# One-hots of a token dispatch built from ranks, wide selections, column-quarter gate logits and waits in a planned order

## Chip, core and metric

The kernel runs on one core of a Trainium2 chip. Times are microseconds (us) of one execution, measured on the device. A lower time is better. The engines are TensorE (PE in the profile, PEld for its weight loads), VectorE (DVE), ScalarE (ACT), GpSimd (POOL) and SyncE (SP, which issues most of the DMAs).

## What is computed

Three parts stand one behind the other, all in float32. S is 576, B is 4, so there are 2304 tokens of 512 values.

```python
# 1. attention, 8 heads of 64, mask by blocks of 64 positions
x = softmax(mask(q @ k.T / 8)) @ v
# 2. a token mix: xk, xr are blends of x and the row before it
k = relu(xk @ w_k);  v = (k * k) @ w_v
y = sigmoid(xr @ w_r) * v
# 3. an expert layer with 8 experts
logits = y @ w_gate;  gate = sigmoid(y @ w_local)
for each batch, for each token in order:
    e = argmax(logits) if first token or gate < 0.5 else the expert of the token before
    out = softmax(logits)[e] * (relu(y @ w1[e]) @ w2[e])
```

## The kernel before

**Attention** goes by 68 units (a batch, a head and a half of its queries, and one unit for the first 64 queries of a batch). **The mix** goes by 9 groups of 256 tokens (`mix_stream`): 96 products with w_k (`acc<-xh,wkh` and the like in the profile), 24 with w_r (`acc<-wrh,xh`), 48 with w_v (`acc<-wvh,kkh`). Each float32 operand is split into a high and a low part, so a product is three matmuls. **The expert layer** goes by slots of 128 tokens of one expert (`slot`): a gather of 128 rows of y by an index list (POOL's indirect DMA, `gidx`), loads of w1 and w2 of that expert, splits of both into high and low parts (ACT writes the high part, DVE the low one: `attr`, `wkh`, `wvh`, `kkh` and their partners, 8 instructions of 128x1024 on each engine for a slot), transposes, two products, a scatter (`sidx`). 19 slots always run, and three small ones of 32 rows (`small_slot`) are put in between at the places of `BEFORE`. A tile's gathered rows are split too: `wrh` on ACT and `wrl` on DVE, three times a slot.

**Which token goes where** is worked out on the chip. After a tile of 128 tokens leaves the mix, `flip` transposes it and `logits` multiplies it with the 9 gate columns (`wg`): four float32 matmuls, each with 128x128 of the tile as stationary operand. `route_group` finds the expert of each token, a one-hot over the experts (`o_all`), and by a triangular product the token's rank within its expert (`rank_all`). After 7 groups `dispatch(True)` gives out the first 7 slots, and after 9 groups `dispatch(False)` the others and the small ones. It works out where each expert's slots begin (`base`, a multiple of 128), so that base plus rank is a position: its upper part is the slot, its lower 7 bits the row. To turn positions into index lists it takes, for each of 14 or 18 tiles, a one-hot of the row (`d_lh`), a one-hot of the slot (`d_sel`), the latter times three values of the token (`d_rhs`: its number and a two-part weight), and one matmul that adds them into one bank (`pinv`). Then `gidx`, `sidx` and `pslot` are read out of it.

**The order** on each engine is fixed ahead by a planner: every call is recorded with its cost, and `schedule` is a list scheduler that takes, for the engine that comes free first, the ready instruction with the lowest `prio` (the length of the work that hangs on it). Everything that is not of the expert layer stands ahead of it by `prio -= 1e5`. Nearly all instructions thus carry the line of the recording helper (L273 before), so the profile is read by tiles. Buffers are rings; `acc` has two banks, shared by all products of the mix.

## Time and profile before

| | us |
|---|---|
| median of 3 runs | 810.71 (809.32 to 812.0) |
| the profiled execution, its own time | 808.18 |
| its span in the profile | 806.4 |

The profiled execution lies 2.5 us under the median. Busy shares of the span: PE 96%, DVE 76%, ACT 66%, POOL 37%. A busy share is an average over stages: attention to about 137 us, attention beside the mix to 477 us, the end of the mix to 525.5 us, the expert layer to 796 us, and the last scatter.

### The profile page before, as it was taken

How to read it: one execution, taken by the hardware profiler on the slowest of the kernel's cores; microseconds unless marked ns; L12 is line 12 of the kernel's file. 1: busy time of each engine (PE TensorE's matmuls, PEld its weight loads, DVE VectorE, ACT ScalarE, POOL GpSimd, SP SyncE). 2: the span in 40 equal slices, each digit the busy share in tenths (PEclk: the TensorE clock that was granted, in tenths of full speed). 3: DMA queues.
4: the chain of work that ended last, by engine and by line, in shares of the span. 5: the costliest groups of instructions: out<-in, count | busy, mean ns of one | idle time of the engine just before them, and what ended most of it. 6: DMA issues, size and time to landing. Idle time of an engine off the chain costs nothing.

```text
span 806.4 us, 15002 instructions
## 1 busy us (share of the span) xinstructions
PE 778.0 (96%) x5040; PEld 640.3 (79%) x5040; DVE 609.6 (76%) x1346; ACT 535.3 (66%) x1156; POOL 299.9 (37%) x275
## 2 busy tenths in 40 slices
PE   8999999999999999999999997999989999999994
PEld 8665798988888989898998986767867777767773
DVE  6986767775789869576785479699999986866840
ACT  3888566983578946265893525469769977867841
POOL 3343585533656427345452332222121521312200
PEclk9999999999999999999999999899999999999998
DMA  8574312211233202201310005111475287695300
GB/s 216 161 211 153 106 57 82 88 45 35 77 92 99 72 17 83 76 28 37 99 45 14 14 27 209 40 39 40 144 248 197 66 275 268 213 327 187 120 15 23
DMA packets 40466, 87.62 MB, mean 109 GB/s; under 512 B 6540, under 2 KB 10640, under 8 KB 40384
## 3 DMA queue, kind: packets, MB, share of 16 engines
q1 hardware_dynamic: 37152, 76.71, 29.6%
q0 software_dynamic: 3232, 9.90, 3.5%
q8 instruction: 41, 0.67, 0.4%
q14 instruction: 41, 0.34, 0.1%
HBM read 131.68 MB, written 9.90 MB: 176 GB/s over the span
## 4 chain that ended last, share of the span: by engine, by line
PE 67%; issue 11%; DVE 11%; DMA 6%; ACT 2%; POOL 1%; SPq 1%; POOLq 0%; ACTq 0%; DVEq 0%
PE acc L273 38%; PE s L273 12%; PE psT L273 9%; PE av L273 6%; DMA out<-xm,sidx 2%; PE acc L1379 1%; DVE wvl L273 1%; DVE attr L273 1%; DVE xm L273 1%; DMA out<-v,ssum 1%; DVE wrl L273 1%; DMA wraw<-in_w 1%; DMA x<-in_w 1%; ACT attr L273 1%; DVE relu L273 1%
## 5 line engine op out<-in xcount | busy, mean ns | idle before, releaser
L273 DVE TENSOR_REDUCE nm<-s 128x1 f32<-128x576 f32 (+4 forms) x132 | 67.7, 547 | 24.2 <-ACT s L273 22.9
L273 PE MATMUL acc<-xh,wkh 128*128 128x256 f32 x288 | 82.1, 295 | 0.9 <-ACT xh L273 0.6
L273 PE MATMUL acc<-xl,wkh 128*128 128x256 f32 x288 | 82.0, 293 | 0.1
L1236 POOL DMA_INDIRECT out<-xm,sidx x19 | 26.3, 1383 | 147.6 <-ACT xm L273 124.9
L273 PE MATMUL acc<-xh,wkl 128*128 128x256 f32 x288 | 80.7, 289 | 0.0
L273 POOL TENSOR_TENSOR attr<-qk,attr 64x512 fp32r<-64x512 f32 (+1 forms) x48 | 65.7, 1368 | 37.8 <-ACT attr L273 30.3
L273 PE MATMUL av<-attr 128*128 128x256 f32 (+3 forms) x336 | 77.4, 288 | 0.8 <-ACT x L273 0.3
L273 DVE TENSOR_TENSOR attr<-psT,attr 64x256 fp32r<-64x256 f32 (+2 forms) x120 | 63.1, 526 | 17.1 <-ACT attr L273 14.7
L273 POOL TENSOR_TENSOR kkl<-relu,kkh 128x512 fp32r<-128x512 f32 x36 | 47.7, 1329 | 61.9 <-ACT kkh L273 53.6
L273 PE MATMUL s<-attr 128*128 128x288 f32 (+3 forms) x288 | 67.1, 300 | 0.6 <-ACT ea L273 0.6
L273 POOL TENSOR_TENSOR xl<-xm,xh 128x512 fp32r<-128x512 f32 x36 | 46.8, 1301 | 49.7 <-ACT xh L273 45.9
L273 ACT ACTIVATE attr<-psT 64x256 fp32r<-64x256 f32 (+2 forms) x120 | 53.0, 463 | 10.4 <-PE psT L273 9.5
L273 PE MATMUL acc<-attr,wrh 128*128 128x512 f32 x160 | 56.7, 405 | 1.1 <-ACT wrh L273 1.1
L273 ACT ACTIVATE xh<-xm 128x512 fp32r<-128x512 f32 x36 | 22.7, 631 | 52.0 <-DVE xm L273 51.9
L273 PE MATMUL acc<-wvh,kkh 128*128 128x512 f32 x144 | 56.6, 414 | 0.0
L273 PEld LDWEIGHTS acc<-xh,wkh 128*128 128x128 f32 x288 | 53.9, 191 | 2.9 <-ACT xh L273 0.9
L273 PEld LDWEIGHTS av<-attr 128*128 128x128 f32 (+1 forms) x336 | 51.5, 166 | 5.3 <-DVE x L273 0.7
L273 PE MATMUL acc<-wvl,kkh 128*128 128x512 f32 x144 | 55.5, 407 | 0.0
L273 PE MATMUL acc<-wvh,kkl 128*128 128x512 f32 x144 | 55.5, 408 | 0.0
L273 PEld LDWEIGHTS acc<-xl,wkh 128*128 128x128 f32 x288 | 54.2, 191 | 1.1 <-POOL xl L273 0.4
L273 PEld LDWEIGHTS acc<-xh,wkl 128*128 128x128 f32 x288 | 54.1, 191 | 0.4
L273 PE MATMUL psT<-ident,eb 128*128 128x128 f32 (+1 forms) x288 | 54.3, 278 | 0.0
(347 smaller groups left out, 2392.8 us busy)
## 6 DMA issues: line engine op xcount, KB each, us to landing
x<-in_w SPq DMA_DIRECT2D x76, 512.0 KB
eb<-in_w SPq DMA_DIRECT2D x38, 512.0 KB
qk<-in_qk SPq DMA_DIRECT2D x24, 544.0 KB
qk<-in_w SPq DMA_DIRECT2D x19, 512.0 KB
d<-in_w SPq DMA_DIRECT2D x19, 512.0 KB
wraw<-in_w SPq DMA_DIRECT2D x24, 256.0 KB
y_dram<-th SPq DMA_DIRECT2D x18, 256.0 KB
v<-in_v SPq DMA_DIRECT2D x28, 160.0 KB
```

Of the source, the lines that this page charges most:

```text
L273: o[2](*o[3], **o[4])
L1236: plan.add("pool", "scatter", lambda: nc.gpsimd.indirect_dma_start(out=out, out_offset=bass.IndirectOffsetOnAxis(ap=at.bitcast(U32), axis= ...
L1379: plan.warm = lambda: pe.matmul(first[:, 0:128], ones, ones, start=True, stop=True)
```

## The change

- **One-hots from ranks.** Since `base` is a multiple of 128, the row is the rank's lower 7 bits. `dispatch` builds all row one-hots from `rank_all` first, once a tile, in bf16, and keeps them: tiles 0 to 15 in the two `wraw` buffers, 16 and 17 in a new tile `hots`. The second dispatch builds four and reuses 14.
- **Wide selections.** One instruction gives the slot one-hots of all 14 tiles (6 tiles in the second dispatch), another multiplies them with the token's values. The values are five bf16 parts (token number in two, weight in three), so the matmuls are bf16 with 5w columns, and three sums put the parts together.
- **Logits.** The gate's weights, padded to 32 columns, are the stationary operand. Four matmuls, one for each 128 of the 512 values, write one quarter of the partitions each; ACT copies the bank to `lt`, PE transposes it, and DVE sums the four parts into `lg` (before, a copy).
- **The planner** lets ACT, DVE and POOL stand idle for at most 300 ns (and half of the instruction at hand) where an instruction that is much more urgent comes ready within that time. The second dispatch has the rank `late`, which loses the lead over the expert layer. The small slots move from places 10, 13 and 15 to 9, 12 and 18.

```diff
-BEFORE = (EARLY + 3, EARLY + 6, EARLY + 8)
+BEFORE = (EARLY + 2, EARLY + 5, EARLY + 11)
...
+FIRM, AHEAD, URGENT = ("act", "dve", "pool"), 300.0, 2000.0
...
-            i = heapq.heappop(b if b and (not a or b[0] < a[0]) else a)[1]
+            mine = b if b and (not a or b[0] < a[0]) else a
+        if e in FIRM and soon[e]:
+            r, j = soon[e][0]
+            if r < t + min(AHEAD, 0.5 * ops[mine[0][1]][2]) and prio[j] < mine[0][0] - URGENT:
+                free[e] = r
+                continue
+        i = heapq.heappop(mine)[1]
...
-        start, order = schedule([(o[0], o[5], o[6], o[8], o[9], o[7][0] != "ffn") for o in ops], until if self.warm else -1, 54.0)
+        start, order = schedule([(o[0], o[5], o[6], o[8], o[9], o[7][0] not in ("ffn", "late")) for o in ops], until if self.warm else -1, 54.0)
...
-    wg = cst.tile([128, 4, NE + 1], F32, name="wg")
+    wg = cst.tile([128, 4, ROWS], F32, name="wg")
+    pool.memset(wg, 0.0)
...
-            pl = aux()
-            for c in range(4):
-                pe.matmul(pl[:, 0:NE + 1], box["yT"][:, c * 128:c * 128 + 128], wg[:, c, :],
-                          start=(c == 0), stop=(c == 3))
-            dve.tensor_copy(lg[:, j, :], pl[:, 0:NE + 1])
+            pl, yt = aux(), box["yT"]
+            def issue():
+                for c in range(4):
+                    nc.tensor.matmul(pl[c * ROWS:c * ROWS + ROWS, 0:128], wg[:, c, :],
+                                     yt[:, c * 128:c * 128 + 128], start=True, stop=True)
+            plan.add("pe", "tiles", issue, outs=[pl[:, 0:128]], ins=[wg, yt], hold=230.0)
+            lt = ring(m1, "lt", [128, 128], F32, 1)
+            act.copy(lt, pl[:, 0:128])
+            pe.transpose(pl[:, 128:256], lt, ident)
+            dve.reduce_sum(lg[:, j, :], pl[:, 128:256].rearrange("p (c e) -> p e c", e=ROWS)[:, 0:NE + 1, :],
+                           axis=AX.X)
...
-    vals = rt.tile([128, NT, 3], F32, name="vals")
+    vals = rt.tile([128, NT, 5], BF16, name="vals")
+    hots = rt.tile([128, 2, 128], BF16, name="hots")
     es = rt.tile([1, SLOTS + 1], F32, name="es")
     dve.memset(es[:, 0:1], -1.0)
+    def hot(t):
+        if t >= 16:
+            return hots[:, t - 16, :]
+        x = buffers(a1, "wraw", [128, 512], F32, 2)[1 + t // 8].bitcast(BF16)
+        return x[:, t % 8 * 128:t % 8 * 128 + 128]
...
+        if not early:
+            plan.rank = ("late", 0, 0)
...
+        for t in ((slice(0, 12), slice(12, 14)) if early else (slice(14, 16), slice(16, 18))):
+            ri, rf = (small(x, [128, 12], dt)[:, 0:t.stop - t.start] for x, dt in (("ri", I32), ("rf", F32)))
+            dve.tensor_copy(ri, rank_all[:, t])
+            dve.tensor_scalar(ri, ri, 127, None, op0=ALU.bitwise_and)
+            dve.tensor_copy(rf, ri)
+            for i in range(t.start, t.stop):
+                dve.tensor_scalar(hot(i), iota128, rf[:, i - t.start:i - t.start + 1], None, op0=ALU.is_equal)
...
-        phr = small("phr", [128, NT], F32R)[:, ts]
-        dve.tensor_copy(phr, p_all[:, ts])
-        dve.tensor_scalar(vals[:, ts, 0], tok[:, ts], 1.0, None, op0=ALU.add)
-        dve.tensor_copy(vals[:, ts, 1], f(phr))
-        dve.tensor_tensor(vals[:, ts, 2], p_all[:, ts], f(phr), op=ALU.subtract)
+        v, x = vals[:, ts, :], f(small("phr", [128, NT], F32R)[:, ts])
+        y = posi[:, 0:v.shape[1]]
+        dve.tensor_scalar(y, tok[:, ts], 1.0, None, op0=ALU.add)
+        for i, mask in enumerate((0x7FFFFFF0, 15)):
+            z = x.bitcast(I32)
+            dve.tensor_scalar(z, y, mask, None, op0=ALU.bitwise_and)
+            dve.tensor_copy(v[:, :, i], z)
+        dve.tensor_copy(v[:, :, 2], p_all[:, ts])
+        dve.tensor_tensor(x, p_all[:, ts], v[:, :, 2], op=ALU.subtract)
+        dve.tensor_copy(v[:, :, 3], x)
+        dve.tensor_tensor(v[:, :, 4], x, v[:, :, 3], op=ALU.subtract)
...
-        for t in range(nt):
-            lh = ring(rt, "d_lh", [128, 128], F32R, 2)
-            dve.tensor_scalar(lh, iota128, pmd[:, 0, t:t + 1], None, op0=ALU.is_equal)
-            sel = ring(rt, "d_sel", [128, 22], F32, 2)[:, 0:w]
-            dve.tensor_scalar(sel, iota25[:, j0:j0 + w], pmd[:, 1, t:t + 1], None, op0=ALU.is_equal)
-            rhs = ring(rt, "d_rhs", [128, 66], F32R, 3)[:, 0:3 * w].rearrange("p (k w) -> p k w", k=3)
-            dve.tensor_tensor(rhs, sel.unsqueeze(1).to_broadcast([128, 3, w]),
-                              vals[:, t, :].unsqueeze(2).to_broadcast([128, 3, w]), op=ALU.mult)
-            pe.matmul(pinv[:, 0:3 * w], lh, rhs, start=(t == 0), stop=(t == nt - 1))
-        inv = small("inv", [128, 66])[:, 0:3 * w].rearrange("p (k w) -> p k w", k=3)
-        dve.tensor_copy(inv, pinv[:, 0:3 * w].rearrange("p (k w) -> p k w", k=3))
+        k = nt if early else 6
+        for t0 in range(0, nt, k):
+            t1 = slice(t0, t0 + k)
+            sel = small("sel", [128, 6 * 22], BF16)[:, 0:k * w].rearrange("p (t w) -> p t w", w=w)
+            dve.tensor_tensor(sel, iota25[:, j0:j0 + w].unsqueeze(1).to_broadcast([128, k, w]),
+                              pmd[:, t1].unsqueeze(2).to_broadcast([128, k, w]), op=ALU.is_equal)
+            rhs = small("rhs", [128, 6 * 110], BF16)[:, 0:k * 5 * w].rearrange("p (t i w) -> p t i w", i=5, w=w)
+            dve.tensor_tensor(rhs, sel.unsqueeze(2).to_broadcast([128, k, 5, w]),
+                              vals[:, t1, :].unsqueeze(3).to_broadcast([128, k, 5, w]), op=ALU.mult)
+            for t in range(k):
+                pe.matmul(pinv[:, 0:5 * w], hot(t0 + t), rhs[:, t].rearrange("p i w -> p (i w)"),
+                          start=(t0 + t == 0), stop=(t0 + t == nt - 1))
...
+        inv = small("inv", [128, 110])[:, 0:5 * w].rearrange("p (k w) -> p k w", k=5)
+        dve.tensor_copy(inv, pinv[:, 0:5 * w].rearrange("p (k w) -> p k w", k=5))
+        dve.tensor_tensor(inv[:, 0, :], inv[:, 0, :], inv[:, 1, :], op=ALU.add)
         dve.tensor_scalar(sidx[st], inv[:, 0, 0:n], -1.0, None, op0=ALU.add)
         dve.tensor_scalar(gidx[st], inv[:, 0, 0:n], -1.0, 0.0, op0=ALU.add, op1=ALU.max)
-        dve.tensor_tensor(pslot[st], inv[:, 1, 0:n], inv[:, 2, 0:n], op=ALU.add)
+        dve.tensor_tensor(inv[:, 1, :], inv[:, 2, :], inv[:, 3, :], op=ALU.add)
+        dve.tensor_tensor(inv[:, 1, :], inv[:, 1, :], inv[:, 4, :], op=ALU.add)
+        dve.tensor_copy(pslot[st], inv[:, 1, 0:n])
```

On DVE, from the cast of the positions (`d_pmd`) to the first index list (`gidx`), before. One tile's three selection instructions repeat, two tiles at a time, with weight splits (`attr<-...`) between them:

```order
L273 CAST d_pmd_185<-d_posi_184 128x2x14
L273 COPY lg_159<-s_0_133 128x9
L273 TENSOR_SCALAR d_sel_189<-iota_103,d_pmd_185 128x8
...
L273 TENSOR_SCALAR d_lh_187<-iota_104,d_pmd_185 128x128
L273 TENSOR_TENSOR d_rhs_191<-d_sel_189,vals 128x24
...
L273 TENSOR_TENSOR attr<-qk_131,attr 128x1024
...
L273 TENSOR_TENSOR attr<-x_0_119,attr 128x1024
L273 COPY d_inv_194<-av_140 128x24
L273 TENSOR_TENSOR wkl<-x_0_121,wkh 128x1024
L273 TENSOR_SCALAR gidx_109<-d_inv_194 128x7
```

The same place in the changed kernel (the instructions of `vals` and two of `xm` are left out):

```order
L282 CAST d_pmd_189<-d_posi_188 128x14
L282 TENSOR_SCALAR d_posi_188<-tok 128x14
L282 TENSOR_TENSOR d_sel_191<-iota_103,d_pmd_189 128x112
...
L282 SCALAR_TENSOR_TENSOR relu_127<-relu_127 128x512
...
L282 TENSOR_TENSOR d_rhs_169<-d_sel_191,vals 128x560
L282 SCALAR_TENSOR_TENSOR xm_129<-d_128,mu_r,x_1_123 128x256
...
L282 TENSOR_TENSOR evi_106<-es 1x7
...
L282 COPY d_inv_192<-av_141 128x40
...
L282 TENSOR_SCALAR gidx_109<-d_inv_192 128x7
```

The 42 selection instructions have become two, and no weight split stands ahead of `gidx` any more; `evi`, the list of experts that the weight loads wait for, now stands behind the selection (before, ahead of `d_pmd`).

On ACT, around the first two weight splits (`attr<-eb`), before:

```order
L273 ACTIVATE relu_126<-acc_151 128x512
L273 ACTIVATE kkh_156<-relu_126 128x512
L273 ACTIVATE attr<-eb_146 128x1024
L273 ACTIVATE attr<-eb_147 128x1024
L273 ACTIVATE relu_126<-acc_151 128x512
L273 ACTIVATE attr<-qk_131 128x1024
```

And in the changed kernel (`th<-acc` reads the first product with w_r out of its bank):

```order
L282 ACTIVATE relu_127<-acc_152 128x512
L282 ACTIVATE kkh_157<-relu_126 128x512
L282 ACTIVATE attr<-eb_147 128x1024
L282 ACTIVATE attr<-eb_148 128x1024
L282 ACTIVATE kkh_157<-relu_127 128x512
L282 ACTIVATE th_124<-acc_151 128x512
L282 ACTIVATE attr<-qk_132 128x1024
```

The reads of the products with w_k now all stand ahead of the two splits; the last `kkh` and the first `th` stand behind them.

On DVE, around the second index list (`gidx_110`, for slots 7 and up), before; the `wrl` behind it is the split of slot 5's gathered rows:

```order
L273 COPY d_inv_194<-s_0_133 128x66
L273 TENSOR_TENSOR xh_152<-x_0_121,kkh_156 128x1024
L273 TENSOR_SCALAR gidx_110<-d_inv_194 128x18
...
L273 COPY d_inv_194<-av_140 128x3
L273 TENSOR_TENSOR wrl<-psT_138,wrh 128x512
```

And in the changed kernel, where the `wrl` ahead of it is that of slot 6:

```order
L282 COPY d_inv_192<-s_0_134 128x110
L282 TENSOR_TENSOR wrl<-psT_140,wrh 128x512
...
L282 TENSOR_TENSOR wkl<-x_0_122,wkh 128x1024
L282 TENSOR_SCALAR gidx_110<-d_inv_192 128x18
```

Counted in slots, the second index list has moved back by more than one.

## Rows read from the trace of the kernel before

**Rows 1.** The page: span and instructions.

```profile
span 806.4 us, 15002 instructions
```

**Rows 2.** Windows by stage: length, busy us of each engine (instructions), clock, DMA share, GB/s.

```profile
137.00:477.00 340.00, 337.51 (x2362) 301.06 (x2360) 248.17 (x638) 218.40 (x585) 156.81 (x131) 0.99 0.18 57
477.00:525.50 48.50, 40.80 (x231) 34.67 (x230) 40.67 (x120) 24.33 (x33) 14.79 (x10) 0.89 0.32 115
525.50:604.20 78.70, 75.84 (x388) 59.66 (x388) 76.21 (x210) 57.20 (x76) 15.87 (x11) 1.00 0.34 118
604.20:796.00 191.80, 189.66 (x1110) 142.86 (x1110) 140.67 (x140) 141.86 (x190) 42.31 (x30) 1.00 0.53 178
```

**Rows 3.** Timeline of PE, 477 to 525.5: start, us, instruction, [idle before, releaser].

```profile
494.37 0.50 PE L273 MATMUL acc<-wrh,xh 128*128 128x512 f32 x1 [1.38 <-ACT relu L273]
...
501.74 0.68 PE L273 MATMUL av<-d_rhs,d_lh 128*128 128x24 f32 x2 [2.43 <-DVE d_rhs L273]
...
505.05 1.88 PE L273 MATMUL s<-wg,relu 128*128 128x9 f32 x8 [0.68 <-ACT relu L273]
...
525.45 0.74 PE L273 MATMUL acc<-attr,wrh 128*128 128x512 f32 x2 [1.06 <-ACT wrh L273]
```

**Rows 4.** Timeline of DVE, the first selection.

```profile
481.86 0.28 DVE L273 TENSOR_TENSOR d_ob<-o_all,taken 128x112 f32<-128x112 f32 x1
...
484.29 0.68 DVE L273 SCALAR_TENSOR_TENSOR relu<-relu 128x512 f32<-128x512 f32 x1
...
487.13 1.20 DVE L273 CAST d_pmd<-d_posi 128x28 f32<-128x28 int32 x1
...
489.96 0.23 DVE L273 TENSOR_SCALAR d_sel<-iota,d_pmd 128x8 f32<-128x8 f32 x1
...
490.38 0.28 DVE L273 TENSOR_SCALAR d_lh<-iota,d_pmd 128x128 fp32r<-128x128 f32 x1
...
504.26 0.15 DVE L273 TENSOR_SCALAR gidx<-d_inv 128x7 int32<-128x7 f32 x1
```

**Rows 5.** Timeline of ACT: a copy out of PSUM, and the first weight split.

```profile
466.01 0.37 ACT L273 COPY wraw<-av 64x256 f32<-64x256 f32 x1
...
491.42 1.06 ACT L273 ACTIVATE attr<-eb 128x1024 fp32r<-128x1024 f32 x1 [0.72 <-DMA eb<-in_w]
```

**Rows 6.** Timeline of PE, one tile's logits and the next instruction.

```profile
444.82 1.06 PE L273 MATMUL acc<-wg,relu 128*128 128x9 f32 x8
...
445.74 0.37 PE L273 MATMUL acc<-xl,wkh 128*128 128x256 f32 x1
```

**Rows 7.** Timeline of PE, a column-quarter product (line 1319) between full ones.

```profile
672.50 0.40 PE L273 MATMUL s<-wkl,wrh 128*128 128x512 f32 x1
...
672.74 0.40 PE L273 MATMUL acc<-attr,wrl 128*128 128x512 f32 x1
...
673.06 0.65 PE L1319 MATMUL av<-wraw,x 128*32 128x128 f32 x16
...
673.74 0.40 PE L1319 MATMUL av<-th,x 128*32 128x128 f32 x8
...
674.07 0.66 PE L273 MATMUL psT<-ident,ea 128*128 128x128 f32 x4
...
674.49 0.48 PE L273 MATMUL s<-wkh,wrl 128*128 128x512 f32 x1
```

**Rows 8.** Timeline of PE, the longest wait after 525.5.

```profile
604.18 0.50 PE L273 MATMUL s<-kkh,wrh 128*128 128x512 f32 x1 [2.09 <-ACT xm L273]
```

**Rows 9.** Timeline of DVE: x splits of slots 0 and 7, the second gather list.

```profile
525.96 0.68 DVE L273 TENSOR_TENSOR wrl<-psT,wrh 128x512 fp32r<-128x512 f32 x1
...
592.19 0.17 DVE L273 TENSOR_SCALAR gidx<-d_inv 128x18 int32<-128x18 f32 x1
...
623.30 0.69 DVE L273 TENSOR_TENSOR wrl<-psT,wrh 128x512 fp32r<-128x512 f32 x1
```

More of the change, by code (lines that the diff above doesn't have):

```diff
@@ L313, in load_constants @@
         sp.dma_start(wg[:, :, 0:NE], a["w_gate"].rearrange("(c p) e -> p c e", p=128))
-        sp.dma_start(wg[:, :, NE:], a["w_local"].rearrange("(c p) e -> p c e", p=128))
+        sp.dma_start(wg[:, :, NE:NE + 1], a["w_local"].rearrange("(c p) e -> p c e", p=128))
     o_all = cst.tile([128, NT, NE], F32, name="o_all")
@@ L932, in to_row @@
                 pe.transpose(v["pk"][0:1, j * 128:j * 128 + 128], v["key"][:, j:j + 1], ident)
-            scan = ring(rt, "scan", [1, GT], F32, 1)
+            scan = ring(rt, "d_rhs", [128, 6 * 110], BF16, 1).bitcast(F32)[0:1, 0:GT]
             init = 0.0 if scan_prev[0] is None else carry
@@ L1108, in dispatch @@
             dve.tensor_tensor(posf, posf, far, op=ALU.add)
-        posi = small("posi", [128, 2, NT], I32)[:, :, 0:nt]
-        dve.tensor_tensor(posi[:, 0, :], posf, rank, op=ALU.add)
-        dve.tensor_scalar(posi[:, 1, :], posi[:, 0, :], 7, None, op0=ALU.logical_shift_right)
-        dve.tensor_scalar(posi[:, 0, :], posi[:, 0, :], 127, None, op0=ALU.bitwise_and)
-        pmd = small("pmd", [128, 2, NT])[:, :, 0:nt]
+        posi = small("posi", [128, NT], I32)[:, 0:nt]
+        dve.tensor_tensor(posi, posf, rank, op=ALU.add)
@@ L1114, in dispatch @@
+        dve.tensor_scalar(posi, posi, 7, None, op0=ALU.logical_shift_right)
+        pmd = small("pmd", [128, NT])[:, 0:nt]
         dve.tensor_copy(pmd, posi)
         ts = slice(0, nt) if early else slice(EG * 2, NT)
-        phr = small("phr", [128, NT], F32R)[:, ts]
-        dve.tensor_copy(phr, p_all[:, ts])
-        dve.tensor_scalar(vals[:, ts, 0], tok[:, ts], 1.0, None, op0=ALU.add)
-        dve.tensor_copy(vals[:, ts, 1], f(phr))
-        dve.tensor_tensor(vals[:, ts, 2], p_all[:, ts], f(phr), op=ALU.subtract)
+        v, x = vals[:, ts, :], f(small("phr", [128, NT], F32R)[:, ts])
@@ L1139, in dispatch @@
+        dve.tensor_tensor(inv[:, 1, :], inv[:, 1, :], inv[:, 4, :], op=ALU.add)
+        dve.tensor_copy(pslot[st], inv[:, 1, 0:n])
         if not early:
             dve.tensor_scalar(gidx_s, inv[:, 0, n:m], -1.0, 0.0, op0=ALU.add, op1=ALU.max)
-            lh = ring(rt, "d_lh", [128, 128], F32R, 2)
+            lh = flat(hots).bitcast(F32)
             dve.tensor_copy(lh.rearrange("p (t r) -> p t r", r=ROWS),
@@ L1145, in dispatch @@
             pr = aux()
-            pe.matmul(pr[:, 0:3 * SMALLS], f(lh), inv[:, :, n:m], start=True, stop=True)
+            pe.matmul(pr[:, 0:2 * SMALLS], lh, inv[:, 0:2, n:m], start=True, stop=True)
             dve.tensor_scalar(sidx_s, pr[:, 0:SMALLS], 4.0, quarter, op0=ALU.mult, op1=ALU.add)
-            dve.tensor_copy(inv[:, 0, 0:SMALLS], pr[:, SMALLS:2 * SMALLS])
-            dve.tensor_tensor(pslot_s, inv[:, 0, 0:SMALLS], pr[:, 2 * SMALLS:3 * SMALLS], op=ALU.add)
+            dve.tensor_copy(pslot_s, pr[:, SMALLS:2 * SMALLS])
     def units():
```

2 lines of the change are left out of this document (1 added, 1 removed).

## Prediction, before the changed kernel was timed

> **What bounds the kernel now.** The span is 806.4 us [rows 1]; the execution's own time is 808.2 us, 1.8 more, and the median of the runs 2.5 above that. The first view is the table of windows by stage. From 137 to 477 us PE is busy 337.5 of 340 us, while DVE has 248 and ACT 218 [rows 2]: there PE sets the pace, and what leaves PE shortens the stage. From 525.5 on PE is busy again (75.8 of 78.7 and 189.7 of 191.8 us), though in the first of these stretches DVE, with 76.2 of 78.7, is as full as PE [rows 2]. The odd stretch lies between, 477 to 525.5 us: PE has 40.8 of 48.5 us and a mean granted clock of 0.89, where the stages around it have 0.99 and 1.00 [rows 2].
>
> The second view is PE's timeline there. It waits 1.38 us for ACT's read of a product, then 2.43 us for the selection of the first dispatch (`d_rhs`, DVE), later 1.06 us for the split of slot 0's rows [rows 3]. Behind the 2.43 us the logits take 1.88 us for what takes 1.06 elsewhere [rows 3, 6]: after the waits PE runs at the lower of its two levels, 1.2 instead of 2.4 GHz. The third view, DVE's timeline, says why the selection is late: from the cast of the positions at 487.13 to `gidx` at 504.26 pass 17.1 us [rows 4], in which DVE does 14 times three small instructions, with weight splits between.
>
> So the sum has three terms: PE work taken out of the saturated stage, the loss in 477 to 525.5, and what the expert layer gains or loses.
>
> **Term 1, the logits.** A tile's eight passes start at 444.82 and the next instruction at 445.74: 0.92 us [rows 6]. No logits of the new form are in the trace, but the small slots have the same shape of product (stationary 128x32, 128 columns, column quarters). There 32 passes start at 673.06, the last eight at 673.74: 0.028 us apart. The full product ahead of them would have freed PE at 672.98 (0.24 after 672.74, as the one before it), and the next one starts at 674.07, about 0.10 after the last pass could end [rows 7]. So entry and exit cost 0.18 us, and eight passes 0.23: 0.41. The added transpose costs a quarter of four, (674.49 - 674.07) / 4 = 0.105 [rows 7]. A tile falls from 0.92 to 0.52, 0.40 saved.
>
> The Trainium skill, "TensorEngine Tiling (Array Packing)", section "Theoretical Speedup", gives up to 4x for a dimension of at most 32, by which the block alone would be 0.92 / 4 = 0.23; its section "Key Properties" says that a change of tiling mode drains the engine. The 0.18 us at the edges agree with the second and speak against counting the first in full: by the 4x alone the term for 14 tiles would be 14 x (0.92 - 0.23 - 0.105) = 8.2 us.
>
> By the rows, 14 of the 18 tiles lie in the saturated stage: 14 x 0.40 = 5.6 us. What it adds on ACT, a copy of 128 columns from PSUM, is bounded by 0 and the 0.37 us of a copy of 256 columns [rows 5]; at 0.3, 18 are 5.4 us, on an engine idle for 120 us of that stage [rows 2]. If ACT set the pace this would cost up to those 5.4 us; the idle share says that it doesn't. DVE's copy becomes a sum of 36 values, below the 0.28 us of a 112-wide instruction [rows 4], hidden likewise. The chain of a tile grows by a copy and a transpose, under 1 us; nothing waits for it before the last tiles. I take 5 of the 5.6 us, with 0 as the lower bound.
>
> **Term 2, the first dispatch.** A tile's selection takes 0.42 us of DVE (489.96 to 490.38) [rows 4], 14 of them 5.9. In their place come one instruction of 112 elements (0.28, as `d_ob`) and one of 560, bounded by 0.28 and 1.06 (the 1024-wide split) [rows 4, 5] and nearest to the 512-wide one: 0.7 [rows 4]. To these come eight to ten small ones for the values and sums, at 0.15 at most 1.5. The row one-hots, each at most 0.28 (`d_lh`) [rows 4], 14 of them 3.9 at most and nearer 2.8 pipelined, are made ahead, in the gaps that DVE has while it waits for the last ranks. Five weight splits of 1.1 us and the waits for PE between the one-hots leave the path too. What stays behind the cast is two squares of 0.6, two or three `xm` of 0.4, the matmuls and some small ones: about 6 us for 17.1. `gidx` should come 11 us sooner. Against it, `evi` goes behind the selection, so the weight loads start some 4 us later than now; now the first split waited 0.72 us for its load at 491.42 [rows 5].
>
> What PE gets of these 11 us. Its loss in the stretch is 48.5 - 40.8 = 7.7 us of waits [rows 2], and of the clock's missing 0.11 x 48.5 = 5.3 us the part that falls on work, which I put at 3.5: 11.2 together. Its work also shrinks, by two logits (0.8) and 14 selection matmuls, now bf16 (0 to 0.1 each; 0.05 taken): 1.5. New waits: the order puts the first `th` on ACT behind two splits whose loads are late. The mix has two banks, so the first product with w_v must wait for that `th`, which I work out to come 2 us after PE wants the bank; and slot 0's split on ACT stands behind four or five splits of the next weights, which the end of the mix frees, as now (1.06 us) [rows 3]. So 3 us of new or remaining waits: 11.2 + 1.5 - 3 = 9.7, taken as 10. Bounds: 13 without new waits, 4 if the loads or the ACT queue hold the mix as long as the selection did.
>
> **Term 3, the expert layer.** PE saves two logits (0.8) and 18 selection matmuls (0.05 each, 0.9). The 2.09 us wait at 604 [rows 8], behind a stretch in which DVE was full with the second dispatch, may go: DVE loses 18 times at least 0.42 us and gets back four one-hots and six wide instructions, about 5, so 3 us less. Against that stands that the first products begin sooner with less in stock. By the order, 13 weight splits stood ahead of slot 0's rows on DVE and now 9: four splits, 4.5 us, that DVE must make up while it is full. Seven slots took 97.3 us from 525.96 to 623.30 [rows 9], 13.9 each. Between +3.8 (all gains, no cost) and -3 (no wait goes, the whole stock lost) I take +1. The small slots move; their places cost nothing now but short waits, and I take 0.
>
> The planner's short waits moved few instructions of the attention stage by more than a few places on any engine; at 2.5 us of waits of PE from 137 to 477 [rows 2] there is little to gain: 0, between -3 and +2.
>
> **Sum.** 5 + 10 + 1 = 16 us: 808.2 - 16 = 792.2 for the profiled execution, 794 to 795 for a median of such runs; I say 794.
>
> **Rivals.**
> (a) *The second list comes too late.* It now stands behind slot 6's split. Before, it came at 592.19 and slot 7's split at 623.30, 31 us ahead [rows 9]. Now a slot's length of about 12.4 us (48 products of 0.24 and twelve transposes of 0.105 [rows 7]) must hold the list, the gather and slot 7's transposes, which I estimate at 9. Each us beyond the 3 to 4 us of slack is one of PE, and more by the clock. It decides against the change from 20 us on: with DVE 24 us behind at slot 6, 794 + 20 = 814. DVE's 3 us less work speak against, its missing stock for it.
> (b) *The first stretch stays long.* The loads, 4 us later, and ACT's queue take the place of the selection, and term 2 falls to 4: 800. For it speaks the wait on a load at 491.42 [rows 5]; against it, that the two reads PE waits for most stand ahead of the splits now.
> (c) *PE's saved work turns into waits* in the mix stage, because ACT's copies hold its two banks: term 1 is 0, 799. Against: 120 us of idle ACT [rows 2].
> (d) *DVE limits slots 1 to 4*, at -3 for term 3: 798, or 803 with (c).
> (e) *Nothing comes of it*: the selection is short, but PE, in its fixed order, waits for another thing as long, and (c) holds: 809 to 811.
> (f) *Better*: the waits at 604 and those of the mix go too, 786 to 788.
>
> **Chances.** Forecast, 788 to 800 with (c) or (d) alone in part: 0.66. (b): 0.12. (c) and (d) in full: 0.06. (f): 0.07. (e): 0.03. (a) to the point of a loss: 0.06. A difference of 0.3% (2.4 us) is about what can be told from no change: faster 0.91, same 0.03, slower 0.06. The range reaches from the better case to (b) and (d) with (c): 786 to 804.
>
> **What would show it.** Right: logits of eight passes with 0.4 us to the next instruction; no wait of PE over 2 us for the selection between the first `d_sob` and slot 0's first product; `gidx` ahead of the first `attr` split; that stretch 10 us shorter, its granted clock over 0.95; the stage before it 5 us shorter. Wrong: PE waits for `th` or `kkh` behind weight splits for more than 3 us, waits on slot 7's gather, or a DVE without gaps up to slot 7 with PE waiting for `wrl` or its partners. The forecast fails most easily in term 2, since ACT's queue there rests on the landing of loads that I did not see in that place.

## The result and the profile after

The changed kernel takes 801.87 us (median of 6 runs, 799.13 to 803.61) against 811.36 us before (6 runs): a ratio of 0.9885, 95% interval 0.9858 to 0.9913. The forecast was 794 in a range of 786 to 804: faster, as said, but 9.5 us by the medians where 16.7 were forecast (810.71 - 794). The profiled execution took 800.13 us, 8.05 less than the one of before, half of the 16 that the prediction added up for it; the spans differ by 8.0 [rows 1].

```profile
span 798.4 us, 15016 instructions
```

To say where the 8 us came from, both kernels are cut at the same three instructions: the first logits, the first product with `d_sob`, and slot 0's first product; the last cut is the end of PE's last product. The windows of the kernel before (columns as in [rows 2]):

```profile
140.56:477.18 336.62, 334.13 (x2338) 297.87 (x2337) 244.88 (x630) 214.94 (x574) 154.99 (x130) 0.99 0.18 56
477.18:525.45 48.27, 40.57 (x230) 34.48 (x226) 40.45 (x119) 24.28 (x33) 14.73 (x10) 0.89 0.32 115
525.45:795.85 270.40, 265.55 (x1497) 202.57 (x1497) 216.93 (x350) 199.03 (x264) 58.22 (x41) 1.00 0.47 160
```

And of the changed kernel:

```profile
140.35:475.37 335.02, 330.00 (x2355) 288.74 (x2355) 244.26 (x640) 217.38 (x589) 155.99 (x129) 1.00 0.18 57
475.37:515.00 39.63, 34.83 (x227) 28.56 (x226) 32.74 (x92) 23.75 (x34) 12.92 (x10) 1.00 0.38 140
515.00:786.24 271.24, 263.87 (x1499) 201.02 (x1499) 219.43 (x323) 199.83 (x267) 55.85 (x40) 0.99 0.47 160
```

The mix stage gained 1.6 us where 5 were expected, the first dispatch 8.6 (expected 10), the expert layer lost 0.8 (expected +1), and from PE's last product to the end the kernel now takes 798.4 - 786.24 = 12.2 us instead of 806.4 - 795.85 = 10.6, which nobody had counted. With 0.2 at the start that is 8.0.

The mix stage first. PE has 4.1 us less work in it, and 335.02 - 330.00 = 5.0 us without work instead of 2.5. Some of the work is the clock's: before, PE ran at the lower of its two levels from 347.1 to 350.5 us, in the changed kernel nowhere in this stage. The timeline of PE shows a block of the new logits between other work:

```profile
246.27 0.42 PE L903 MATMUL acc<-relu,wg 128*32 128x128 f32 x8
246.63 0.40 PE L282 MATMUL av<-attr 128*64 128x256 f32 x2
```

0.36 us to the next instruction, where the old block took 0.92 [rows 6]. So each block is as short as forecast, and the stage is not. The trace lists what PE waits for here. The largest group, 1.5 us in five places, is the logits product itself, which waits for ACT's copy of the transposed tile, its own input; 0.8 us are waits for the reads behind it (`lt` on ACT, `lg` on DVE).

The first dispatch, on PE's timeline: the 14 selection products in one row, the two waits for `th`, slot 0's first product.

```profile
487.26 0.52 PE L282 MATMUL av<-d_rhs,wraw 128*128 128x40 bf16 x14
...
498.55 0.50 PE L282 MATMUL acc<-wvh,kkh 128*128 128x512 f32 x1 [1.61 <-ACT th L282]
...
504.77 0.51 PE L282 MATMUL acc<-wvh,kkh 128*128 128x512 f32 x1 [1.55 <-ACT th L282]
...
515.00 0.96 PE L282 MATMUL acc<-attr,wrh 128*128 128x512 f32 x3 [0.21 <-ACT wrh L282]
```

The 2.43 us wait for `d_rhs` [rows 3] is gone; 1.61 and 1.55 for `th`, behind ACT's weight splits, have taken its place, and the clock is 1.00 instead of 0.89. In all PE is without work for 4.8 us here, before for 7.7. On DVE the selection now looks like this:

```profile
481.97 0.17 DVE L282 CAST d_pmd<-d_posi 128x14 f32<-128x14 int32 x1
...
482.26 0.27 DVE L282 TENSOR_TENSOR d_sel<-iota,d_pmd 128x112 bf16<-128x112 f32 x1
...
484.53 1.79 DVE L282 TENSOR_TENSOR d_rhs<-d_sel,vals 128x560 bf16<-128x560 bf16 x1
...
490.71 0.16 DVE L282 TENSOR_SCALAR gidx<-d_inv 128x7 int32<-128x7 f32 x1
...
495.77 3.03 DVE L282 TENSOR_TENSOR attr<-eb,attr 128x1024 fp32r<-128x1024 f32 x2 [1.42 <-ACT attr L282]
```

From `d_pmd` to `gidx` it is 8.7 us, not 17.1 [rows 4], and the first weight split comes 5 us behind the list. Of the 17.1 us before, the 42 selection instructions took 8.1 (from the start of each to DVE's next instruction) and five weight splits 5.7; DVE was idle for only 0.8, in one wait for PE. The first split, and that wait:

```profile
492.71 1.22 DVE L273 TENSOR_TENSOR attr<-eb,attr 128x1024 fp32r<-128x1024 f32 x1
...
496.33 0.29 DVE L273 TENSOR_SCALAR d_lh<-iota,d_pmd 128x128 fp32r<-128x128 f32 x1 [0.81 <-PE av L273]
```

In the expert layer the 2.09 us wait at 604 [rows 8] has gone, and a longer one stands at slot 7:

```profile
600.80 0.39 PE L282 MATMUL s<-wkh,wrl 128*128 128x512 f32 x1
606.19 1.12 PE L282 MATMUL psT<-ident,ea 128*128 128x128 f32 x4 [5.01 <-DMA ea<-y_dram,gidx]
...
608.39 0.63 PE L282 MATMUL s<-wkl,wrh 128*128 128x512 f32 x1
608.82 0.58 PE L282 MATMUL s<-wkh,wrl 128*128 128x512 f32 x1
609.23 0.40 PE L282 MATMUL s<-wkh,wrh 128*128 128x512 f32 x1
```

PE waits 5.0 us for slot 7's gathered rows, and for some 3 us behind that a product takes 0.43 us instead of 0.23: the lower clock. The second gather list came at 595.58 us on DVE (592.19 before [rows 9]), but the split of slot 7's gathered rows has moved from 619.29 to 608.24, so 12.7 us lie between the two instead of 27.1. (A slot's three `wrl` are one split of its gathered rows and two of the two halves of its hidden values; the 623.30 of [rows 9] is one of the latter, of slot 6. By the same reading the list stood behind the rows of slot 5 before and stands behind those of slot 6 now: one slot, not more.) The split of slot 7's rows, before:

```profile
619.29 0.69 DVE L273 TENSOR_TENSOR wrl<-psT,wrh 128x512 fp32r<-128x512 f32 x1 [0.46 <-ACT wrh L273]
```

With the list another thing moved, which the prediction didn't name: `evi`, the list of experts by which SP picks the weights of slots 7 and up. DVE wrote it at 555 us before and now at 594:

```profile
594.27 0.16 DVE L282 TENSOR_TENSOR evi<-es 1x18 int32<-1x18 f32 x1
```

SP's weight loads around it, in the changed kernel:

```profile
569.88 21.07 SPq L1305 DMA_DIRECT2D x<-in_w  x3
593.63 0.37 SPq L1305 DMA_DIRECT2D d<-in_w  x1
597.13 0.99 SPq L1305 DMA_DIRECT2D eb<-in_w  x2
```

The first loads behind the new list start at 597.13, in the same microseconds in which the gather (issued at 596.51) has to land.

### The profile page after: what moved, and what is told of

Read it like the earlier page. It is cut to its first block, busy times and chain, and to the rows that moved or that the text cites. A ratio compares the mean times of both kernels' runs of the same rounds, so it can differ in the third digit from the quotient of the medians.

```text
span 798.4 us, 15016 instructions
## 1 busy us (share of the span) xinstructions
PE 766.2 (96%) x5069; PEld 623.3 (78%) x5069; DVE 599.9 (75%) x1301; ACT 538.4 (67%) x1174; POOL 297.6 (37%) x276
## 4 chain that ended last, share of the span: by engine, by line
PE 65%; issue 10%; DMA 10%; DVE 6%; ACT 6%; POOL 2%; SPq 1%; POOLq 0%; ACTq 0%
PE acc L282 35%; PE s L282 13%; PE psT L282 8%; PE av L282 5%; DMA qk<-in_qk 2%; DMA x<-in_w 2%; ACT attr L282 2%; DMA out<-xm,sidx 2%; PE acc L1428 2%; DMA th<-in_w 2%; DMA ea<-y_dram,gidx 1%; DVE attr L282 1%; ACT relu L282 1%; ACT ea L282 1%; POOL ea L1276 1%
## 5 line engine op out<-in xcount | busy, mean ns | idle before, releaser
L282 POOL TENSOR_TENSOR kkl<-relu,kkh 128x512 fp32r<-128x512 f32 x36 | 47.8, 1328 | 58.0 <-ACT kkh L282 45.1
L282 PE MATMUL acc<-attr,wrh 128*128 128x512 f32 x160 | 60.7, 411 | 0.2 <-ACT wrh L282 0.2
L282 PE MATMUL psT<-ident,ea 128*128 128x128 f32 (+2 forms) x256 | 51.7, 276 | 5.4 <-DMA ea<-y_dram,gidx 5.0
L282 PE MATMUL acc<-wvh,kkh 128*128 128x512 f32 x144 | 53.4, 409 | 3.2 <-ACT th L282 3.2
L282 DVE TENSOR_TENSOR wrl<-psT,wrh 128x512 fp32r<-128x512 f32 x57 | 39.2, 688 | 22.3 <-ACT wrh L282 22.1
L282 ACT ACTIVATE relu<-acc 128x512 f32<-128x512 f32 x55 | 32.5, 595 | 32.1 <-PE acc L282 30.8
```

The source lines that it names most:

```text
L282: o[2](*o[3], **o[4])
```

## Experiments

Twelve kernels ran, each timed against the kernel before on the same chip. They ran on several chips, so runs are compared by their ratios to the kernel before (the changed kernel: 0.9885) and by stages rather than by their medians. The stages are the three windows above, then the tail, from the profile of each.

| run | us | ratio (95%) | mix | to slot 0 | experts | tail |
|---|---|---|---|---|---|---|
| before | 811.4 | | 336.6 | 48.3 | 270.4 | 10.6 |
| changed | 801.9 | 0.9885 (0.9858 to 0.9913) | 335.0 | 39.6 | 271.2 | 12.2 |
| 1 no late rank | 808.3 | 0.9988 (0.9967 to 1.0008) | 335.0 | 40.3 | 277.8 | 12.2 |
| 2 third small slot at 17 | 799.8 | 0.9871 (0.9845 to 0.9898) | 336.0 | 40.2 | 270.8 | 10.1 |
| 3 no short waits | 809.6 | 0.9994 (0.9975 to 1.0014) | 337.1 | 47.8 | 268.7 | 12.2 |
| 4 before + logits | 808.7 | 0.9991 (0.9976 to 1.0006) | 336.5 | 48.0 | 270.8 | 10.6 |
| 5 before + planner | 804.5 | 0.9942 (0.9921 to 0.9963) | 331.6 | 43.5 | 277.1 | 10.2 |
| 6 old logits | 799.4 | 0.9883 (0.9857 to 0.9910) | 331.5 | 39.6 | 273.3 | 12.1 |
| 7 tenth of rank, third at 17 | 803.7 | 0.9912 (0.9886 to 0.9938) | 335.1 | 42.0 | 273.5 | 10.8 |
| 8 expert list first | 802.0 | 0.9899 (0.9877 to 0.9921) | 334.2 | 41.0 | 272.3 | 12.2 |
| 9 old logits, third at 17 | 797.8 | 0.9858 (0.9832 to 0.9885) | 331.6 | 40.1 | 273.0 | 10.3 |
| 10 as 9, expert list first | 794.6 | 0.9807 (0.9785 to 0.9829) | 331.4 | 38.6 | 271.1 | 10.3 |
| 11 old passes, new chain | 804.6 | 0.9923 (0.9896 to 0.9951) | 337.9 | 41.9 | 270.7 | 12.2 |
| 12 before + planner + places | 804.4 | 0.9920 (0.9891 to 0.9949) | 331.6 | 43.3 | 276.2 | 12.3 |

**1. The late rank undone.** Is slot 7's wait the price of the late rank, and worth undoing?

```diff
-... o[7][0] not in ("ffn", "late")) for o in ops] ...
+... o[7][0] != "ffn") for o in ops] ...
```

> The changed kernel with one part undone: the second dispatch keeps its lead over the expert layer, so the second gather list stands behind slot 1's split of rows instead of behind the first of slot 6's three. Theory G (the list comes too late): in the changed kernel PE waited 5.0 us for slot 7's gathered rows and ran about 3 us at the lower clock behind that; both go, and the time falls by 5 to 7 us against the changed kernel's 801.9, to 795 to 797. Rival D (DVE is the limit there, and the late rank is what keeps slots 0 to 3 supplied): the wait goes, but some 12 us of dispatch instructions now stand ahead of the splits of slots 0 to 2, PE waits for wrl or for weights' low parts instead, and the time is 800 to 806.

Slower than the changed kernel by 1% and beyond the range of either theory: 808.3. The direction is D's. The wait for slot 7's rows goes, and the expert layer is 6.6 us longer all the same. PE's timeline:

```profile
540.91 0.46 PE L282 MATMUL s<-d_rhs,wraw 128*128 128x110 bf16 x6 [0.70 <-DVE d_rhs L282]
542.66 0.50 PE L282 MATMUL s<-xh,wrh 128*128 128x512 f32 x1 [1.29 <-DVE xh L282]
...
592.91 0.79 PE L282 MATMUL s<-wkh,wrh 128*128 128x512 f32 x1 [2.55 <-ACT wrh L282]
```

The dispatch, with its lead, takes DVE from slots 0 to 2: the first two waits. The third stands behind ACT, whose split waited 2.84 us for the load of its weights (`qk<-in_w`) at 590.37; that this too comes of the rank is not shown. The late rank is worth more than the wait it brings.

**2. The last small slot one place earlier.**

```diff
-BEFORE = (EARLY + 2, EARLY + 5, EARLY + 11)
+BEFORE = (EARLY + 2, EARLY + 5, EARLY + 10)
```

> The changed kernel with one number changed: the third small slot stands before slot 17 instead of before slot 18, the last. Theory T (the last scatter waits for the small slot's scatter to land): the changed kernel's last product was read out at 787.0 us but its scatter was issued at 790.0, behind a scatter of 128 columns issued at 786.3. With the small slot earlier the last scatter is issued 0.3 us after its rows are ready, the stretch from PE's last product to the end falls from 12.2 to 10.6 us or less, and the time by 1.6 to 2.7 us: 799 to 800. Rival (the place costs nothing: the end of the span is a landing time that hangs on neither): no difference, 801.5 to 802.5.

POOL's end in the changed kernel, where the last rows were read out of PSUM by ACT from 786.32 to 787.0:

```profile
786.28 0.99 POOL L1415 DMA_INDIRECT out<-v,ssum  x1 [9.19 <-ACT v L282]
790.00 0.98 POOL L1285 DMA_INDIRECT out<-xm,sidx  x1 [2.73 <-DMA out<-v,ssum]
```

And in this run, where ACT's last read began at 791.02:

```profile
785.51 0.99 POOL L1415 DMA_INDIRECT out<-v,ssum  x1 [2.54 <-ACT v L282]
791.98 0.98 POOL L1285 DMA_INDIRECT out<-xm,sidx  x1 [5.48 <-ACT xm L282]
```

The last scatter no longer waits for the small slot's to land, and the tail is 2.1 us shorter (T). By the times alone (0.9871 against 0.9885) the intervals overlap, and so they do for run 9 against run 6 (0.9858 against 0.9883), where the tail falls by the same step, from 12.1 to 10.3 us. What shows it is the tail.

**3. The short waits switched off.**

```diff
-FIRM, AHEAD, URGENT = ("act", "dve", "pool"), 300.0, 2000.0
+FIRM, AHEAD, URGENT = (), 300.0, 2000.0
```

> The changed kernel with the planner's short waits switched off. By the order four weight splits then stand ahead of the first gather list on DVE, and the list of experts ahead of the selection, as before the change. Theory F1 (the short waits moved the splits behind the list, the rest of the change cut the selection): gidx comes 4 to 5 us later than 490.7, the loads some 6 us sooner; slot 0's first product comes 3 to 5 us later than 515.0, total 803 to 806. Rival F2 (the short waits do little for the first list, since the loads then come later by as much, and they cost PE 2.5 us of waits in the mix): the mix stage up to the first d_sob product shortens by 2 to 3 us, the stretch behind it stays, total 798 to 800.

All of the gain is gone, more than F1 had expected, and F2 falls. The two wide instructions are there, and the list is as late as before. DVE:

```profile
490.20 0.16 DVE L282 CAST d_pmd<-d_posi 128x14 f32<-128x14 int32 x1
491.69 1.23 DVE L282 TENSOR_TENSOR attr<-eb,attr 128x1024 fp32r<-128x1024 f32 x1 [1.33 <-ACT attr L282]
...
502.49 0.74 DVE L282 TENSOR_TENSOR d_rhs<-d_sel,vals 128x560 bf16<-128x560 bf16 x1
...
506.85 0.17 DVE L282 TENSOR_SCALAR gidx<-d_inv 128x7 int32<-128x7 f32 x1
```

16.7 us from `d_pmd` to `gidx`, of which eight splits of weights take 9.1: five between `d_pmd` and `d_rhs`, three behind it. DVE is idle for 2.3 us; the only split that waits is the first, 1.33 us for ACT's half.

**4. The new logits alone on the kernel before.**

```diff
-                pe.matmul(pl[:, 0:NE + 1], box["yT"][...], wg[:, c, :], ...)
-            dve.tensor_copy(lg[:, j, :], pl[:, 0:NE + 1])
+            plan.add("pe", "tiles", issue, ...)
+            lt = ring(rt, "d_ob3", [128, 256], F32, 1)[:, 0:128]
+            act.copy(lt, pl[:, 0:128])
+            pe.transpose(pl[:, 128:256], lt, ident)
+            dve.reduce_sum(lg[:, j, :], ...)
```

> The kernel before with the new logits alone (gate weights stationary on column quarters, copy on ACT, transpose, sum on DVE; to make room the scan's row, the copy and the dispatch's comparison table share one buffer). Theory L1 (term 1 of the prediction: 0.4 to 0.46 us of PE for each of 14 tiles, PE sets the pace): the first d_sob product comes 5 us sooner than 477.2 and the time falls by 5 to 6 us, to 805 to 806. Rival L2 (what PE saves in the mix stage turns mostly into waits for ACT's copies, as the 1.8 us that the changed kernel gained up to the first d_sob suggests): 1 to 2.5 us, 809 to 810.

No difference that can be told (0.9976 to 1.0006), and the mix stage is 336.5 us: L1 falls, and even L2's 1 us is not sure. (The copy `lt` shares its buffer with another row of the kernel here, so this is not quite the changed kernel's chain.) PE's work in the stage fell by 3.2 us and its time without work rose by 3.1:

```profile
141.05:477.58 336.53, 330.92 (x2355) 288.89 (x2354) 243.78 (x630) 218.10 (x590) 156.41 (x129) 1.00 0.18 57
```

**5. The planner's part alone.** The kernel before with the short waits and the late rank.

```diff
+FIRM, AHEAD, URGENT = ("act", "dve", "pool"), 300.0, 2000.0
...
+            plan.rank = ("late", 0, 0)
```

> The kernel before with the planner's part alone: the short waits and the late rank of the second dispatch; the 42 selection instructions a tile at a time, the old logits and the old places of the small slots stay. By its order the first gather list stands ahead of all weight splits on DVE, as in the changed kernel. Theory P (the order did it: what made the first list late was the splits ahead of it, each behind its load and ACT, and the selection itself is 6 us of DVE): gidx comes about 5 us later than the changed kernel's 490.7, at 495 to 497, some 8 us sooner than before; slot 0's first product 5 to 8 us sooner than 525.5; total 802 to 805. Rival S (the wide selection did it, and the order only helps where the selection is short): the 42 instructions still take 15 us, PE waits for d_rhs as before, total 807 to 811.

P, and more than P: half of the gain (0.9942), with the old selection. Its 42 instructions stand ahead of all splits, from `d_pmd` at 478.87:

```profile
478.87 0.18 DVE L281 CAST d_pmd<-d_posi 128x28 f32<-128x28 int32 x1
...
488.82 1.24 DVE L281 TENSOR_SCALAR gidx<-d_inv 128x7 int32<-128x7 f32 x1
```

That is 9.95 us, where the two wide instructions and what belongs to them took 8.7; the 42 take 6.4 us of it. So S falls: most of what made the stretch long was what stood between the selection's instructions. The short waits also took 5.0 us from the mix stage, which none of the theories had (the late rank has no part in that: without it, in run 1, the stage is as long as in the changed kernel): PE is without work there for 1.1 us instead of 2.5, and its work is 3.6 us less, with the same products between the marks, at a granted clock of 1.00 instead of 0.99. The stretch at the lower level, 3.4 us before, accounts for 1.7 of that by its half speed; the rest is not traced.

```profile
140.61:472.21 331.60, 330.49 (x2339) 295.60 (x2338) 241.92 (x631) 215.56 (x574) 155.94 (x130) 1.00 0.18 57
```

**6. The changed kernel with the old logits.**

```diff
-            plan.add("pe", "tiles", issue, outs=[pl[:, 0:128]], ins=[wg, yt], hold=230.0)
...
+                pe.matmul(pl[:, 0:NE + 1], box["yT"][:, c * 128:c * 128 + 128], wg[:, c, 0:NE + 1], ...)
+            dve.tensor_copy(lg[:, j, :], pl[:, 0:NE + 1])
```

> The changed kernel with the old logits (eight passes of the tile as stationary operand; no copy, transpose or sum). The first kernel with the new logits alone was 0.7 us faster than before, with an interval that holds zero. Theory L2 (what PE saves in the mix turns into waits for ACT's and DVE's reads of the same bank): 800.5 to 803.5, no difference that can be told from the changed kernel's 801.9. Rival L1 (the saving counts in full once the rest of the order is right): 5 us slower, 806 to 808. In the stage from the first logits to the first d_sob product L2 expects 335 to 336.6 us, L1 340.

By the time L2 (0.9883 against 0.9885), but both were wrong on the stage: it is not as long as with the new logits, it is 3.5 us shorter (331.5), as in run 5:

```profile
140.48:471.98 331.50, 330.31 (x2339) 295.49 (x2338) 245.44 (x643) 215.78 (x574) 156.14 (x130) 1.00 0.18 57
```

So in this order the new logits cost 3.5 us there, nearly all of it PE's time without work (1.2 us here, 5.0 in the changed kernel). PE's work is 330.3 and 330.0 us, though the passes of the 14 tiles take 5.1 us instead of 11.2 (each to PE's next instruction) and the transposes add only 1.5: most of what the passes save comes back in other products, which isn't explained. The expert layer gives 2 of the 3.5 us back in the comparison, so by the ratios the whole comes out even.

**7. A tenth of the lead, and the third small slot at 17.**

```diff
-... o[7][0] not in ("ffn", "late")) ...      prio = [x - 1e5 * o[5] ...]
+... {"ffn": 0.0, "late": 0.1}.get(o[7][0], 1.0)) ...
```

> The changed kernel with the third small slot before slot 17 and with a tenth of the lead for the second dispatch (it was none; the kernel before had the whole). By the order the second gather list then stands behind 16 splits of rows, those of slots 0 to 4 and one of slot 5, instead of 19. Theory G2 (the list needs only one slot more of room; the whole lead, as the run without the late rank showed, takes DVE from slots 0 to 3): the 5.0 us wait of PE for slot 7's rows and the 3 us at the lower clock behind it go, no wait on DVE of more than 1 us comes between slots 0 and 7, and the time is 793 to 796. Rival D2 (DVE is full anyway, so that any earlier place of the list is paid by late splits): 798 to 802.

G2 falls. 803.7 is beyond D2 too, though its interval overlaps that of the changed kernel and its six times spread from 798.5 to 804.3. Counted from slot 0's first product the list came 10 us sooner (70.2 instead of 80.6 us); PE no longer waits for the gather, and waits 3.27 us for ACT's `wrh`. On ACT's timeline that stands behind a split whose load is late:

```profile
596.33 1.06 ACT L282 ACTIVATE wvh<-eb 128x1024 fp32r<-128x1024 f32 x1 [3.18 <-DMA eb<-in_w]
597.29 0.58 ACT L282 ACTIVATE wrh<-psT 128x512 fp32r<-128x512 f32 x1
```

The expert list came at 586.58 here, just ahead of the gather list. It was not the gather alone that the late rank put off.

**8. The list of experts with its lead, the rest late.**

```diff
+        if not early:
+            plan.rank = ("lead", 0, 0)
         pc = aux()
...
             dve.tensor_copy(evi[st][:, 0, n:m], part)
+            plan.rank = ("late", 0, 0)
```

> The changed kernel with one part of the second dispatch given its lead back: the counts and the list of experts, about 30 small instructions up to that list; one-hots, positions, selection and gather list keep the late rank. By the order the expert list then stands behind 4 splits of rows (it came at 594.3 us, just ahead of the gather list), and the gather list stays behind 19. Theory E (the late rank put off the list of experts, by which SP picks the weights of slots 7 and up: the DMA engines stood still from 574 to 590 us and then had to bring the weights and the gathered rows of slot 7 at once): the loads of slot 7's weights start before 580, the gather issued at 596.5 lands 2 to 5 us sooner than at 606.2, the 5.0 us wait falls below 2 and the time to 796 to 799. Rival G (the gather itself is late, its landing takes 7 us whatever else is loaded): the wait stays at 4 to 5 us and the time at 801 to 803.

The mechanism is E's, the time is G's. The expert list comes at 534.5, SP's loads go on through the pause from 570 to 597 us (the changed kernel's DMA share was 0.06 from 577 to 590), and the 5.0 us wait has become 1.39, now for another thing. But PE is without work for 7.5 us in the expert layer, in the changed kernel for 7.4. Among the waits are now two of 1.4 us for ACT's `relu` and more for the weights of the small slots, where DMA has a share of 0.79 (636 to 717 us; 0.82 in the changed kernel):

```profile
602.44 0.66 PE L282 MATMUL psT<-ident,relu 128*128 128x128 f32 x4 [1.39 <-ACT relu L282]
...
684.71 0.63 PE L1371 MATMUL s<-wraw,v 128*32 128x256 f32 x4 [1.29 <-DMA wraw<-in_w]
```

Ahead of slot 0, where the changed kernel waits twice for `th` (1.61 and 1.55 us), there is one wait of 3.33; behind it PE ran at the lower level for 3.4 us, and the granted clock of that stretch is 0.96 instead of 1.00. It is 1.4 us longer. So the time that the gather gave was given back.

**9 and 10. Old logits, third small slot at 17, and then the expert list first.** Edits as in runs 6, 2 and 8.

> The changed kernel with the old logits and the third small slot before slot 17. With theory T the stretch from PE's last product to the end is 10 to 10.6 us instead of 12.2, and the time 1.6 to 2.7 us under the run with the old logits alone (799.4): 796.7 to 797.8. If the place gives nothing: 799 to 800.

> The run before this one with the list of experts given its lead back as well. Theory E: the wait of 3.4 us at slot 7 in the run with the old logits goes with its 3 us at the lower clock, 3 to 5 us under the run before: 792 to 795. Rival G: 796 to 798, as there.

797.8 and 794.6: T holds for the tail (10.3), and with the old logits E holds in the time as well, 0.9858 against 0.9807, with intervals that do not overlap. Of the 3.8 us between the two profiled executions, 1.9 lie in the expert layer, where the waits around slot 7 (2.93 and 0.55) have become one of 1.49, and 1.5 ahead of slot 0. Run 10 beats both kernels; it is 1.9% under the first.

**11. The old passes with the new chain.**

```diff
+            act.copy(lt[:, 0:NE + 1], pl[:, 0:NE + 1])
+            pe.transpose(pl[:, 128:256], lt, ident)
+            dve.reduce_sum(lt[:, 64:64 + NE + 1], ..., axis=AX.X)
             dve.tensor_copy(lg[:, j, :], pl[:, 0:NE + 1])
```

> The run with the old logits (eight passes of the tile as stationary operand), to which only the chain behind them is added: ACT copies the nine columns into lt, PE transposes lt into the same bank, and DVE sums 36 values of it, whose result is not used, before the bank is free. It tells apart why the stage from the first logits to the first d_sob product took 331.5 us with the old logits and 335.0 with the new ones. Theory C (the chain: the shared bank is held for a copy, a transpose and a sum, and PE waits for these and for reads queued behind them): 1.5 us of transposes and 2 to 4 us of waits more, the stage at 335 to 337. Rival M (the column-quarter product itself, whose entries and exits cost as much as its passes save): the transposes alone, the stage at 332.5 to 333.5, and less than 1.5 us of listed waits in it (0.7 with the old logits, 4.7 with the new ones).

C, and beyond its upper edge: 337.9 us. PE has 4.0 us more work and 2.3 more without work than in run 6:

```profile
139.94:477.80 337.86, 334.35 (x2365) 299.28 (x2364) 243.37 (x658) 218.69 (x592) 156.59 (x131) 1.00 0.18 57
```

The chain costs 6.4 us, and the column-quarter passes win 2.8 of them (335.0). Counted from the span's start to the first `d_sob` product it is 5.8 and 2.4, because in run 11 the first logits stand 0.5 us sooner, and 13 products of the attention and the mix that stood ahead of them stand behind. Of the 4.0 us of work the transposes are at most 1.5, and those 13 products about 1.3 by an estimate at 0.1 us each; the rest stays open (the planner's order differs as well). Of the 3.5 us without work 0.8 are listed waits for `lt` and `lg`; the largest others are of the attention's products for DVE (`attr`).

**12. Planner and places, without the wide selection.** Run 5 with the changed kernel's `BEFORE`.

> The run with the planner's part alone (short waits and late rank on the kernel before, 804.5) with the changed kernel's places of the small slots added; against the run with the old logits (799.4) it lacks the one-hots from ranks and the wide selections alone. Theory W (the wide selection is worth 4 us in each dispatch, as the stretches of those two runs suggest: 43.5 and 39.6 us up to slot 0's first product, 277.1 and 273.3 behind it): places give nothing or lose the 2 us of the last scatter, 804 to 807. Rival Q (the places give what was seen behind slot 0, the selection only its 4 us ahead of it): 801 to 803.

W: places change nothing that can be told (804.4 against 804.5), though the tail is longer by the 2 us. The wide selection with its one-hots, run 6 against this one, is worth 5.0 us by the medians and 3.0 by the ratios, 0.9883 against 0.9920, with intervals that overlap; in the profiled executions 3.7 us up to slot 0, and 2.9 behind it.

## Why the prediction came out as it did

**The range held, the sum did not.** 801.87 lies in 786 to 804, but outside 788 to 800, to which the forecast gave 0.66; half of the 16 us came. That the time stayed in the range is in part luck: the planner's short waits, put at 0, gave 5.0 us in run 5 and so covered what the logits lost.

**Term 1 (5 us): the price was right, the saving wasn't there.** A block leaves PE after 0.36 us, as worked out from the small slots (0.41 with its entry). The Trainium skill, "TensorEngine Tiling (Array Packing)", section "Theoretical Speedup", gives up to 4x, by which an estimate of the block is 0.92 / 4 = 0.23; the trace shows 0.36, so the figure of the page is not to be counted in full here. The step that failed is the sentence that the chain grows "by a copy and a transpose, under 1 us; nothing waits for it". Run 4 shows the result (0.1 us gained in the stage), runs 6 and 11 that the chain takes the saving: put behind the old passes it alone makes the stage 6.4 us longer. How it does so is only in part seen. The bank is one of two that the mix's products share, and it is held for the copy, the transpose and the sum; but the listed waits for these come to 0.8 us, the logits product's wait for its own input to 1.5, and the rest lies in the attention's waits and in PE's work. That the hold of the bank is the main cause is not shown. The result is rival (c)'s. It was dismissed for ACT's idle share, and an average of 120 idle microseconds says nothing of a wait for one copy at one place.

The 1.6 us that the stage gained are, by runs 5 and 6, the short waits' 5.0 less the 3.4 that the logits took back. By the other way, the logits first (run 4, 0.1 us) and the short waits last (run 3 against the changed kernel), the latter give 2.1: the two do not simply add. The prediction put the short waits at 0, between -3 and +2, because PE waits only 2.5 us there; they also took out the stretch at the lower clock and gave PE less work, which lay outside its bounds.

**Term 2 (10 us): the size nearly right (8.6), the weight put on the wrong part.** The list came 13.6 us sooner, the clock is 1.00 and no wait is over 2 us. PE's work fell by 5.7 us (3.5 for the clock and 1.5 were taken), its time without work by 2.9: 4.8 us are left where the sum had 3 for all new or remaining waits. The prediction's first reason was 42 instructions against two, and it named the splits in half a sentence ("Five weight splits ... leave the path too"). Run 3 has the two instructions and none of the gain, run 5 the 42 and half of it. What stretched some 10 us to 17 was mostly the splits' own time between the selection's instructions, 5.7 us before and 9.1 in run 3; waits of a split for its load or for ACT had little part (none before, 1.33 us in run 3).

**Term 3 (+1 us): -0.8, by rival (a) at a small price.** PE's work fell by 1.7 us, what the sum had for it, in spite of the stretch at the lower clock, but its time without work rose by 2.5. The wait for slot 7's gather was foreseen, with 20 us as the point from which it decides; it came with 5.0 us and 3 us of half clock. The missing step is that the late rank moves all of the dispatch, the list of experts with it, which starts the loads. Runs 7, 8 and 10 show that both lists hang there. The slot's length was also read from the wrong split: from slot 0's rows to slot 7's it is 93.3 us before (525.96 to 619.29), not 97.3, so 13.3 a slot, and the list was 27.1 us ahead, not 31. DVE as the limit, rival (d), is in part what run 1 shows when the rank is undone.

**The sum left out the tail.** "The small slots move; their places cost nothing now but short waits, and I take 0": the third small slot at the end cost 1.6 us in the profiled execution, and 2.1 came back in run 2.

## What to carry to other kernels

In a fixed order, whatever stands between the links of an urgent chain adds its whole time to it: before making a chain shorter, look at what is interleaved with it. A saving on the busiest engine is only had if what feeds the product and what takes its result keep up: try the new chain behind the old product, as run 11 does, and do not go by the idle share of the engine that copies. When a piece of work is put off, list every output of it: here the gather list had slack, the list of experts that starts the loads had none. And look at the last transfer of a program: a small write just ahead of it can hold it back, here by about 2 us.

## What the runs showed of the hardware

**The start differs between executions.** In the profile of run 2 the granted clock is 0.83 over the first 20 us, where the changed kernel, with the same instructions there, has 1.00. Its first logits come at 143.95 instead of 140.35, and this execution took 802.72 us while its others went down to 797.92:

```profile
0.00:20.00 20.00, 16.15 (x154) 14.68 (x155) 10.98 (x35) 4.29 (x10) 6.17 (x30) 0.83 0.76 204
```

So in this execution 3.6 us were lost before any of the changed work, and stages are better compared from a landmark than from time zero.

**One instruction, two durations.** The wide product `d_rhs` (128x560, bf16) took 1.79 us at 484.53 in the changed kernel and 0.74 in run 3. In the first case POOL ran a product of two tensors beside it:

```profile
484.44 1.28 POOL L282 TENSOR_TENSOR kkl<-relu,kkh 128x512 fp32r<-128x512 f32 x1 [6.52 <-issue]
```

The estimate of 0.7 held for the instruction alone; here it took 1.05 more. But it isn't always DVE that pays. In run 6 the same two instructions start together, DVE's keeps its 0.74 us, and POOL's takes 1.88 instead of 1.28 (run 9 shows the same pair of times):

```profile
481.58 1.88 POOL L282 TENSOR_TENSOR kkl<-relu,kkh 128x512 fp32r<-128x512 f32 x1 [6.72 <-issue]
...
481.59 0.74 DVE L282 TENSOR_TENSOR d_rhs<-d_sel,vals 128x560 bf16<-128x560 bf16 x1
```

What decides which of the two is held up, no run here settles.
